# Attention and feed-forward in one kernel: batch 0 split into two pieces of its queries, with h of the first under the scores of the second

## The chip, the cores and the metric

The kernel runs on one core of a Trainium2 chip. The metric is the device time of one execution in microseconds. Before the change the median was 387.45 us over three runs (387.23 to 388.66). A program of one core has no second die to compare with; all runs that are compared here were in the fast state, that is, within 1.5% of the fastest run of their kernel. Some of them had a slightly lower mean granted TensorE clock than others (0.99 against 1.00), which is said where it matters.

Names in the profile: PE is TensorE, PEld its weight loads, DVE VectorE, ACT ScalarE, POOL GpSimd, SP SyncE.

## The reference

```python
def reference(q, k, v, w_in, w_out):            # q, k, v: 8 x 12 x 448 x 64
    scores = q @ k.transpose(0, 1, 3, 2) / 8
    attn = np.maximum(scores, 0.0) ** 2 / 448
    x = (attn @ v).transpose(0, 2, 1, 3).reshape(3584, 768)
    h = x @ w_in                                # 768 x 2048
    g = np.maximum(h, 0.0) ** 2
    return g @ w_out                            # 2048 x 768
```

There are eight batches of 448 rows. A batch is three units of four heads; a unit's keys come in J = 7 tiles of 64, so a batch has 21 score tiles. h of a batch can't start before its last unit's values are summed, since h sums over all heads.

## The kernel before

Each score tile is four 64x64 matmuls that run at the same time in the four quarters of the PE array. ACT takes relu out of PSUM, DVE squares, and a "value round" of four 64x64 matmuls adds the tile to the unit's output. `visit` is the unit of interleaving: scores of two tiles, then the value rounds of tiles seen two visits earlier. An f tile is 128 of the 2048 columns of h. In the lines of the profile, slot is a PSUM slot, at a score tile after its relu, avt the sum of the value rounds in PSUM, xt the transposed x, hps an accumulator of h, and g the squared relu of h.

```python
def slot(dtype):                       # a PSUM slot of two banks
    slot_no[0] += 1
    third = "mm" not in big and slot_no[0] % 3 == 2 and slot_no[0] < 29
    return (third_p if third else s_p).tile([P, 2, 2048 // size(dtype)], ...)

def score(t, times=1):
    ps = slot(FP32)
    for hh in list(range(2)) * times:  # times is 2 before h exists: the same product twice
        for hp in range(2):
            nc.tensor.matmul(ps[c, hh, 0:S], lhsT=kT[r, j, c], rhs=qT[r, :, c], ...)
    at = at_p.tile([P, 2, S], FP16, ...)
    nc.scalar.activation(out=at, in_=ps[:, :, 0:S], func=AF.Relu, scale=SK)

def visit(tiles, turn=None, lag=2, most=3):
    ...                                # prefetch of later units
    for t in tiles:
        score(t, 1 if "mm" in big else 2)
    later = pe_transpose(turn) if turn is not None else None
    flush()                            # squares on DVE
    av_some(lag, most)                 # value rounds
    ...
```

While batch 0's scores are made there are three slots. Then the third one's two banks become the two accumulators of h, and scores and transpositions share two slots. `pe_transpose` turns q and k of a unit on PE into one slot; copies to SBUF (qT, kT) follow, on DVE for units 0 to 2 and on ACT for units 3 to 5. Later units are transposed by DMA. The beginning is written out by hand, and h of batch 0 is then interleaved with the attention of batch 1:

```python
warm(10)
pe_transpose(0)
for i in range(11):
    visit([t for t in (2 * i, 2 * i + 1) if t < NB0], turn={1: 1, 4: 2, 10: 3}.get(i))
    ...                                # loads of later units and of the weights
f0 = h_group(0, 0)
for _, fn, _ in f0[0:4]:
    fn()
av_some(0, 9)
visit([NB0, NB0 + 1])
seq = [[2, 3], 4, [4, 5], [6, 7], [8, 9], 5, [10, 11], ...]   # visits and transpositions,
...                                    # one behind each of h's 16 groups of 6 matmuls
```

## Time and profile before

| stretch of the kernel before | from, us | to, us |
|---|---|---|
| batch 0's scores, until h goes on without a break | 8.2 | 29.66 |
| h of batch 0 under the attention of batch 1 | 29.66 | 61.38 |
| everything from h of batch 1 on | 61.38 | 385.6 |

The prediction below shows the lines behind the first two rows. The times of the second and third row are starts of h matmuls in the timeline of PE, the third of this one (start, us, then engine, line, operation, tiles, shapes and count):

```profile
61.38 0.93 PE L343 MATMUL hps<-xt,w 128*128 128x448 f16 x4
```

The last row is the same program in both kernels.

### The profile page before, as it was taken

To read this page: it belongs to the slowest core of one execution; us is meant where nothing else is said; L and a number is where in the kernel's file an instruction comes from. 1 tells how busy PE (TensorE), PEld (TensorE's weight loads), DVE (VectorE), ACT (ScalarE), POOL (GpSimd) and SP (SyncE) were. 2 spreads that over 40 slices of the span, in tenths; PEclk is the share of its full clock that TensorE was granted. 3 is DMA by queue.
4 is the path that set the end of the run, shared out by engine and by line. 5 is a ranking of instruction groups with operands and counts; after the bars stand their busy time and mean duration, and the time that the engine had idled before them with its cause. 6 is when DMAs were issued, how large, how long until landed. Compare 5 with 4: busy or idle time off the path is not lost.

```text
span 385.6 us, 7681 instructions
## 1 busy us (share of the span) xinstructions
PE 373.8 (97%) x3160; PEld 187.4 (49%) x3160; DVE 249.8 (65%) x401; ACT 235.9 (61%) x354; POOL 81.2 (21%) x96
## 2 busy tenths in 40 slices
PE   7889999999999999999999999999999999999994
PEld 3554434444554444445555544444555444556652
DVE  2885778999787676568587465566777563244441
ACT  3998874776555886676455578777464684442221
POOL 8544304653203222020113332030000000000001
PEclk9999999999999999999999999999999999999999
DMA  8999995998687994640989757344323300001333
GB/s 122 201 202 205 252 204 150 233 283 193 182 170 191 234 139 125 144 73 2 210 210 174 149 185 168 49 120 73 62 69 83 82 2 0 2 0 45 96 95 94
DMA packets 64482, 50.83 MB, mean 132 GB/s; under 512 B 35712, under 2 KB 60768, under 8 KB 64448
## 3 DMA queue, kind: packets, MB, share of 16 engines
q1 hardware_dynamic: 46672, 33.66, 36.0%
q0 software_dynamic: 17696, 16.58, 26.6%
q8 instruction: 25, 0.41, 0.4%
q10 hardware_dynamic: 80, 0.10, 0.1%
q14 instruction: 9, 0.07, 0.1%
HBM read 45.61 MB, written 11.01 MB: 147 GB/s over the span
## 4 chain that ended last, share of the span: by engine, by line
PE 86%; DVE 6%; ACT 3%; DMA 2%; issue 1%; POOL 1%; POOLq 0%; DVEq 0%; ACTq 0%
PE hps L343 38%; PE ops L497 27%; PE slot L248 9%; PE avt L266 7%; PE slot L497 4%; DVE at L312 2%; ACT at L252 2%; DMA k<-in_k_dram 2%; DVE xt L279 1%; DVE s L403 1%; PE slot L218 1%; ACT qT L210 0%; DVE g L364 0%; ACT kT L210 0%; POOL q L93 0%
## 5 line engine op out<-in xcount | busy, mean ns | idle before, releaser
L343 PE MATMUL hps<-xt,w 128*128 128x448 f16 x768 | 154.3, 353 | 0.3 <-ACT xt L276 0.3
L252 ACT ACTIVATE at<-slot 128x896 f16<-128x896 f32 x168 | 144.1, 920 | 16.0 <-PE slot L248 16.0
L312 DVE TENSOR_TENSOR at<-at 128x896 f16<-128x896 f16 x168 | 106.1, 653 | 33.0 <-ACT at L252 32.4
L343 PEld LDWEIGHTS <-w 128*128 128x128 f16 x768 | 71.2, 98 | 78.2 <-issue 16.9
L358 ACT ACTIVATE g<-hps 128x448 f16<-128x448 f32 x120 | 65.4, 546 | 56.1 <-PE hps L343 51.2
L364 DVE TENSOR_TENSOR g<-g 128x896 f16<-128x896 f16 x63 | 42.6, 677 | 43.8 <-ACT g L358 43.6
L497 PEld LDWEIGHTS <-s 128*128 128x128 f16 x448 | 42.6, 98 | 33.8 <-issue 4.1
L248 PE MATMUL slot<-qT,kT 64*64 64x448 f16 x756 | 53.8, 359 | 1.6 <-ACT kT L210 0.5
L123 POOL CAST qs<-qf 128x896 f16<-128x896 f32 x18 | 20.1, 1115 | 155.9 <-DMA qf<-in_q_dram 120.5
L266 PE MATMUL avt<-at,vt 64*64 64x448 f16 x672 | 47.8, 350 | 1.1 <-DVE xt L279 1.1
L497 PEld LDWEIGHTS <-g 128*128 128x128 f16 x336 | 31.3, 98 | 27.1 <-issue 7.7
L497 PE MATMUL ops<-b,s 128*128 128x384 f16 x192 | 35.2, 326 | 0.9 <-DVE s L403 0.9
L497 PE MATMUL ops<-t,s 128*128 128x384 f16 x192 | 34.6, 326 | 0.2
L279 DVE TENSOR_SCALAR xt<-avt 128x448 f16<-128x448 f32 x46 | 26.6, 618 | 12.6 <-PE avt L266 12.6
L497 PE MATMUL ops<-b,g 128*128 128x384 f16 x192 | 34.7, 326 | 0.0
L425 ACT ACTIVATE u<-ops 128x384 f32<-128x384 f32 x24 | 11.8, 492 | 34.9 <-PE ops L497 25.1
L248 PEld LDWEIGHTS <-kT 64*64 64x64 f16 x756 | 16.5, 105 | 31.8 <-issue 28.5
L266 PEld LDWEIGHTS <-vt 64*64 64x64 f16 x672 | 19.9, 107 | 14.9 <-issue 4.4
L374 POOL DMA_DIRECT2D out_dram<-osb x2 | 1.1, 568 | 121.2 <-ACT osb L460 121.2
L123 POOL CAST ks<-kf 128x896 f16<-128x896 f32 x18 | 23.0, 1277 | 4.9 <-DMA kf<-in_k_dram 4.1
L429 DVE SCALAR_TENSOR_TENSOR osb<-ops,u 128x384 f32<-128x384 f32 x24 | 13.3, 554 | 14.4 <-ACT u L425 10.0
L403 DVE TENSOR_TENSOR s<-g 128x1024 f16<-128x1024 f16 x26 | 19.1, 736 | 0.1
(50 smaller groups left out, 173.2 us busy)
## 6 DMA issues: line engine op xcount, KB each, us to landing
out_dram<-osb SPq DMA_DIRECT2D x52, 192.0 KB, 2.9
qf<-in_q_dram SPq DMA_DIRECT2D x16, 448.0 KB, 5.1
kf<-in_k_dram SPq DMA_DIRECT2D x16, 448.0 KB, 5.8
vt<-in_v_dram POOLq DMA_DIRECT2D x24, 224.0 KB, 4.6
w<-in_moe_w_in_dram POOLq DMA_DIRECT2D x8, 384.0 KB, 11.7
b<-in_moe_w_out_dram POOLq DMA_DIRECT2D x4, 768.0 KB, 17.4
q<-in_q_dram POOLq DMA_DIRECT2D x6, 224.0 KB, 7.8
k<-in_k_dram POOLq DMA_DIRECT2D x6, 224.0 KB, 8.1
```

Source lines behind the costliest of these rows:

```text
L123: ins = nc.gpsimd.tensor_copy(t.rearrange("p j h d -> p h j d"), src.rearrange("p h (j d) -> p h j d", d=D))
L248: nc.tensor.matmul(ps[c, hh, 0:S], lhsT=kT[r, j, c], rhs=qT[r, :, c], start=True, stop=True)
L252: nc.scalar.activation(out=at, in_=ps[:, :, 0:S], func=AF.Relu, scale=SK)
L266: nc.tensor.matmul(ap[hp][64 * hh:64 * hh + 64, 0:S], lhsT=vt[r, hh, j * D:(j + 1) * D], rhs=at[r, hh, :], start=(j == 0), stop=(j == J - 1))
L279: nc.vector.tensor_scalar(out=dst, in0=ap[hp][:, 0:S], scalar1=CX, scalar2=None, op0=ALU.mult)
L312: nc.vector.tensor_mul(at, at, at)
L343: held[:] = [nc.tensor.matmul(cell[0][:, 0:S], lhsT=w1[f // 4][:, m, (f % 4) * P:(f % 4 + 1) * P], rhs=xts[b][:, m, :], start=(m == 0), st ...
L358: nc.scalar.activation(out=g[:, f % 2], in_=cell[0][:, 0:S], func=AF.Relu)
L364: nc.vector.tensor_mul(g, g, g)
L403: op(to[i], x, y)
L429: nc.vector.scalar_tensor_tensor(out=osb[row][:, c], in0=Y[0][:, cc], scalar=CO, in1=keep[nm][:, cc], op0=ALU.mult, op1=ALU.add)
L497: nc.tensor.matmul(acc[0][:, 0:HALF], lhsT=left()[:, f], rhs=right[:, f], start=(fresh and f == 0), stop=(f == KH - 1), skip_group_check=n ...
```

## The change: its intent and the diff

In the kernel before, PE has little of use to do while ACT takes batch 0's relus. The change makes scores of the first 256 queries for all heads first (HEAD). h of these queries can then start, and the scores of the other 192 queries (TAIL) are made under it. Two tiles of a piece share a slot (2 x 256 or 2 x 192 columns in a bank). h is done in 16 blocks of two f tiles and one piece, 12 matmuls each. The order of all visits and h blocks up to h of batch 1 is fixed by hand. All relus of HEAD's h blocks are on ACT; of TAIL's, every second one is on DVE.

```diff
+    WHOLE, HEAD, TAIL = (0, J), (0, 4), (4, J)
+    av_order: deque = deque()
+    for piece in (HEAD, TAIL):
+        av_order.extend((t, piece) for t in range(NU * J))
+    av_order.extend((t, WHOLE) for t in range(NU * J, NUN * J))
...
+    def score(parts, times=1):
         ps = slot(FP32)
+        used = sum(width(piece) for _, piece in parts)
...
+                    nc.tensor.matmul(
+                        ps[c, hh, o:o + w], lhsT=kT[r, j, c],
+                        rhs=qT[r, piece[0]:piece[1], c], start=True, stop=True)
...
+        nc.scalar.activation(out=atv, in_=ps[:, :, 0:used], func=AF.Relu, scale=SK)
...
+    hd, tl = pairs(0, HEAD, range(20)), pairs(0, TAIL, range(4))
+    order0 = hd[:3] + tl[:1] + hd[3:7] + tl[1:] + hd[7:] + [[(20, HEAD), (4, TAIL)]]
+    for i, parts in enumerate(order0):
+        visit([parts], turn={2: 1, 7: 2}.get(i))
...                                   # loads: w1's first blocks now before q, k of unit 3
+    run(h0[0:4])
+    av_some(0, 9)
+    visit(next(tails))
+    run(h0[4:])
+    h_head(1)
+    visit(next(tails))
+    h_head(2)
+    pe_transpose(3)
+    visit(next(tails))
+    h_head(3)
+    visit(next(tails))
...
+    h_head(4)
+    visit(next(b1))
+    h_head(5)
+    visit(next(b1))
+    pe_transpose(4)
+    h_tail(0)
+    for i in range(1, 6):
+        visit(next(b1))
+        if i == 4:
+            pe_transpose(5)
+        h_tail(i)
...                                   # h_head(6), h_head(7), h_tail(6), h_tail(7), a visit before each
```

More of the change, by code (lines that the diff above doesn't have):

```diff
@@ L191, in slot @@
         slot_no[0] += 1
-        third = "mm" not in big and slot_no[0] % 3 == 2 and slot_no[0] < 29
+        third = "mm" not in big and slot_no[0] % 3 == 1
         return (third_p if third else s_p).tile(
@@ L224, in pe_transpose @@
         qkt[n] = ts
-        if n == 3:
-            return lambda: (copy(0, 0), copy(1, 0))
         if n > 0:
@@ L229, in pe_transpose @@
             copy(1, n < 3)
-        return None
     xts: dict = {}
@@ L236, with width, av_round @@
     now = [0]
-    av_order: deque = deque(range(NUN * J))
     avt = [None]
-    def score(t, times=1):
-        n, j = divmod(t, J)
-        qT, kT = qkt[n]
-        ps = slot(FP32)
-        for hh in list(range(2)) * times:
-            r = slice(64 * hh, 64 * hh + 64)
-            for hp in range(2):
-                c = slice(64 * hp, 64 * hp + 64)
-                nc.tensor.matmul(
-                    ps[c, hh, 0:S], lhsT=kT[r, j, c], rhs=qT[r, :, c],
-                    start=True, stop=True)
-        at = at_p.tile([P, 2, S], FP16, name="at", tag="at")
-        nc.scalar.activation(out=at, in_=ps[:, :, 0:S], func=AF.Relu, scale=SK)
-        ats[t] = at
-        seen[t] = now[0]
-    def av_round(t):
+    WHOLE, HEAD, TAIL = (0, J), (0, 4), (4, J)
[3 more added lines that the diff above has]
+    av_order.extend((t, WHOLE) for t in range(NU * J, NUN * J))
+    def width(piece):
+        return (piece[1] - piece[0]) * PW
+    def score(parts, times=1):
+        ps = slot(FP32)
+        used = sum(width(piece) for _, piece in parts)
+        at = at_p.tile([P, 1024], FP16, name="at", tag="at")
+        atv = at[:, 0:2 * used].rearrange("p (g w) -> p g w", w=used)
+        o = 0
+        for t, piece in parts:
+            n, j = divmod(t, J)
+            qT, kT = qkt[n]
+            w = width(piece)
+            for hh in list(range(2)) * times:
+                r = slice(64 * hh, 64 * hh + 64)
+                for hp in range(2):
+                    c = slice(64 * hp, 64 * hp + 64)
+                    nc.tensor.matmul(
+                        ps[c, hh, o:o + w], lhsT=kT[r, j, c],
+                        rhs=qT[r, piece[0]:piece[1], c], start=True, stop=True)
+            ats[t, piece] = atv[:, :, o:o + w]
+            seen[t, piece] = now[0]
+            o += w
+        nc.scalar.activation(out=atv, in_=ps[:, :, 0:used], func=AF.Relu, scale=SK)
+        return at[:, 0:2 * used], parts
+    def av_round(t, piece):
         n, j = divmod(t, J)
         b, u = divmod(n, NU)
-        vt, at = vts[n], ats.pop(t)
+        w = width(piece)
+        z = piece[0] * PW
+        assert all((t, piece) not in parts for _, parts in due)
+        vt, at = vts[n], ats.pop((t, piece))
         if j == 0:
@@ L266, in av_round @@
                 nc.tensor.matmul(
-                    ap[hp][64 * hh:64 * hh + 64, 0:S],
+                    ap[hp][64 * hh:64 * hh + 64, 0:w],
                     lhsT=vt[r, hh, j * D:(j + 1) * D], rhs=at[r, hh, :],
@@ L270, in av_round, with av_some @@
         if j == J - 1:
-            if u == 0:
+            if b not in xts:
                 xts[b] = x_p.tile([P, NM, S], FP16, name="xt", tag="xt")
             for hp in range(2):
-                dst = xts[b][:, 2 * u + hp, :]
+                dst = xts[b][:, 2 * u + hp, z:z + w]
                 if b < 2 and u == NU - 1 and hp == 0:
                     nc.scalar.activation(
-                        out=dst, in_=ap[hp][:, 0:S], func=AF.Copy, scale=CX)
+                        out=dst, in_=ap[hp][:, 0:w], func=AF.Copy, scale=CX)
                 else:
                     nc.vector.tensor_scalar(
-                        out=dst, in0=ap[hp][:, 0:S],
+                        out=dst, in0=ap[hp][:, 0:w],
                         scalar1=CX, scalar2=None, op0=ALU.mult)
-    def av_some(lag=2, most=3):
-        done = 0
-        while av_order and done < most:
-            t = av_order[0]
-            if t not in seen or seen[t] > now[0] - lag:
+    def av_some(lag=2, most=3.1):
+        done = 0.0
+        while av_order:
+            key = av_order[0]
+            done += width(key[1]) / S
+            if done > most or key not in seen or seen[key] > now[0] - lag:
                 break
             av_order.popleft()
-            av_round(t)
-            done += 1
-            if t % J == J - 1:
+            av_round(*key)
+            if key[0] % J == J - 1:
                 break
@@ L303, in prefetch, with visit, whole @@
         dma_transpose(m)
-    copies: deque = deque()
     due: list = []
     def flush():
-        for at in due:
+        for at, _ in due:
             nc.vector.tensor_mul(at, at, at)
         due.clear()
-    def visit(tiles, turn=None, lag=2, most=3):
+    def visit(slots, turn=None, lag=2, most=3.1):
         now[0] += 1
-        for t in tiles:
-            if t % J == 0 and t >= NPE * J:
-                prefetch(t // J + 2)
-        for t in tiles:
-            score(t, 1 if "mm" in big else 2)
-        later = pe_transpose(turn) if turn is not None else None
+        for parts in slots:
+            for t, _ in parts:
+                if t % J == 0 and t >= NPE * J:
+                    prefetch(t // J + 2)
+        new = [score(parts, 1 if "mm" in big else 2) for parts in slots]
+        if turn is not None:
+            pe_transpose(turn)
         flush()
         av_some(lag, most)
-        if later:
-            later()
-        due.extend(ats[t] for t in tiles)
+        due.extend(new)
         if "mm" not in big:
             flush()
+    def whole(ts):
+        return [[(t, WHOLE)] for t in ts]
     gts: dict = {}
@@ L352, in run @@
                 g = gts[pr][:, f0:f0 + 2, z:z + S]
-                if b == 0 and (f % 2 == 1 or f == 0) and f < 14:
-                    nc.vector.tensor_scalar(
-                        out=g[:, f % 2], in0=cell[0][:, 0:S],
-                        scalar1=0.0, scalar2=None, op0=ALU.max)
-                else:
-                    nc.scalar.activation(
-                        out=g[:, f % 2], in_=cell[0][:, 0:S], func=AF.Relu)
+                nc.scalar.activation(
+                    out=g[:, f % 2], in_=cell[0][:, 0:S], func=AF.Relu)
                 flush()
-                if b == 0 and f == NF - 1:
-                    due.append(g)
-                elif f % 2 == 1:
+                if f % 2 == 1:
                     nc.vector.tensor_mul(g, g, g)
@@ L367, in h_group, with h_piece, step, run @@
         return [(0.1892, step(m), m == 0) for m in range(NM)]
+    def h_piece(piece, i):
+        w = width(piece)
+        z = piece[0] * PW
+        cell = [None]
+        def step(e, m):
+            def run():
+                if e == 0 and m == 0:
+                    cell[0] = big["mm"].tile([P, 512], FP32, name="hps", tag="mm")
+                f = 2 * i + e
+                held[:] = [nc.tensor.matmul(
+                    cell[0][:, e * w:(e + 1) * w],
+                    lhsT=w1[f // 4][:, m, (f % 4) * P:(f % 4 + 1) * P],
+                    rhs=xts[0][:, m, z:z + w], start=(m == 0), stop=(m == NM - 1))]
+                if e == 0 or m < NM - 1:
+                    return
+                if 0 not in gts:
+                    gts[0] = g_p.tile([P, NF, 2 * S], FP16, name="g", tag="g")
+                g = gts[0][:, 2 * i:2 * i + 2, z:z + w]
+                src = cell[0][:, 0:2 * w].rearrange("p (e w) -> p e w", w=w)
+                if piece == TAIL and i % 2 == 0:
+                    nc.vector.tensor_scalar(
+                        out=g, in0=src, scalar1=0.0, scalar2=None, op0=ALU.max)
+                else:
+                    nc.scalar.activation(out=g, in_=src, func=AF.Relu)
+                flush()
+                if piece == TAIL and i == NF // 2 - 1:
+                    due.append((g, ()))
+                else:
+                    nc.vector.tensor_mul(g, g, g)
+            return run
+        return [step(e, m) for e in range(2) for m in range(NM)]
     def store(row, osb, c, eng, eng2=None):
@@ L529, with pairs, run, h_head @@
     NB0 = NU * J
+    def pairs(b, piece, ts):
+        parts = [(b * NB0 + t, piece) for t in ts]
+        return [parts[i:i + 2] for i in range(0, len(parts), 2)]
     warm(10)
     pe_transpose(0)
-    for i in range(11):
-        visit([t for t in (2 * i, 2 * i + 1) if t < NB0],
-              turn={1: 1, 4: 2, 10: 3}.get(i))
-        if i == 0:
-            load16(3)
+    hd, tl = pairs(0, HEAD, range(20)), pairs(0, TAIL, range(4))
+    order0 = hd[:3] + tl[:1] + hd[3:7] + tl[1:] + hd[7:] + [[(20, HEAD), (4, TAIL)]]
+    for i, parts in enumerate(order0):
+        visit([parts], turn={2: 1, 7: 2}.get(i))
+        if i == 2:
             load_w1(0)
             load_w1(1)
+            load16(3)
+            load_w1(2)
+        if i == 4:
+            load16(4)
             load_v(3)
-        if i == 2:
-            load16(4)
-            load_w1(2)
+            load_w1(3)
             load_v(4)
-        if i == 5:
+        if i == 8:
             load16(5)
-            load_w1(3)
             load_v(5)
             load_qk(6, nc.gpsimd)
+    first.close()
+    big["mm"] = ctx.enter_context(tc.tile_pool(name="mmps", bufs=2, space=PSUM))
+    def run(steps):
+        for fn in steps:
+            fn()
+    def h_head(*ii):
+        for i in ii:
+            run(h_piece(HEAD, i))
+    def h_tail(*ii):
+        for i in ii:
+            run(h_piece(TAIL, i))
+    tl = pairs(0, TAIL, range(5, 21))
+    tails = iter([tl[i:i + 2] for i in range(0, 8, 2)])
+    b1 = iter([whole([NB0 + t for t in ts]) for ts in
+               [(2 * i, 2 * i + 1) for i in range(10)] + [(20,)]])
+    h0 = h_piece(HEAD, 0)
+    run(h0[0:4])
[9 more added lines that the diff above has]
+    visit(next(tails))
     load_v(6)
@@ L554 @@
     load_qk(7, nc.gpsimd)
-    first.close()
-    big["mm"] = ctx.enter_context(tc.tile_pool(name="mmps", bufs=2, space=PSUM))
-    f0 = h_group(0, 0)
-    for _, fn, _ in f0[0:4]:
-        fn()
+    h_head(4)
[6 more added lines that the diff above has]
+        visit(next(b1))
+        if i == 4:
+            pe_transpose(5)
+        h_tail(i)
+    visit(next(b1))
+    h_head(6)
+    visit(next(b1))
+    h_head(7)
+    visit(next(b1))
+    h_tail(6)
+    visit(next(b1))
+    h_tail(7)
+    visit([])
     av_some(0, 9)
-    visit([NB0, NB0 + 1])
     T_G = NM * 0.1892
@@ L570 @@
     events = []
-    seq = [[2, 3], 4, [4, 5], [6, 7], [8, 9], 5, [10, 11], [12, 13], [14, 15],
-           [16, 17], [18, 19], [20], []]
-    for i, ts in enumerate(seq):
-        at = (2.5 + i) * T_G
-        if isinstance(ts, int):
-            events.append((at, lambda n=ts: pe_transpose(n)))
-        else:
-            events.append((at, lambda ts=ts: visit([NB0 + t for t in ts])))
-    events.append((T_H, lambda: av_some(0, 9)))
     def ready():
@@ L597 @@
             ts = [t0 + 2 * i, t0 + 2 * i + 1]
-            events.append((at0 + i * gap, lambda ts=ts: visit(ts)))
+            events.append((at0 + i * gap, lambda ts=ts: visit(whole(ts))))
         at0 = end
@@ L601 @@
         events.append((at0 + 0.3 + i, lambda: visit([])))
-    steps = [(0.1892, None, False)] * 4 + f0[4:]
-    for f in range(1, NF):
-        steps += h_group(0, f)
+    steps = []
     for f in range(NF):
@@ L613 @@
         steps += o_steps(pr)
-    clock = 0.0
+    clock = T_H
     ev = deque(sorted(events, key=lambda e: e[0]))
```

## The prediction

> **What bounds the kernel now.** I began with the summary of engines and then cut the span into stretches, because the change touches only the beginning: everything from h of batch 1 on stands in the same order in both kernels. The columns are the stretch, its length, then busy time and instruction count of PE, PEld, DVE, ACT and POOL, the granted clock, the share of the DMA engines and GB/s.
>
> ```profile
> PE 373.8 (97%) x3160; PEld 187.4 (49%) x3160; DVE 249.8 (65%) x401; ACT 235.9 (61%) x354; POOL 81.2 (21%) x96
> ...
> 8.00:26.00 18.00, 15.30 (x285) 8.73 (x278) 15.02 (x28) 16.67 (x21) 9.28 (x14) 1.00 1.24 200
> 27.40:61.40 34.00, 32.85 (x337) 14.46 (x334) 22.82 (x42) 26.57 (x36) 8.96 (x12) 1.00 1.24 229
> 61.40:92.00 30.60, 29.77 (x228) 14.09 (x224) 30.32 (x37) 21.48 (x34) 17.97 (x16) 1.00 0.98 214
> ```
>
> Over the whole span PE is the bound. But from 8 to 26 us, where batch 0's scores are made, ACT is busy 16.67 of 18 us: each score is issued twice there, so half of PE's score time does nothing. From 27.4 to 61.4 (h of batch 0 with attention of batch 1) PE leads, and ACT has 7.4 us in hand. From 61.4 to 92 DVE is full.
>
> The chain that ended last (start, us, what) shows the handover:
>
> ```profile
> 4.77 6.12 DMA k<-in_k_dram
> ...
> 24.98 0.97 ACT at L252
> 26.00 0.97 PE slot L218 x28
> 26.97 0.50 PE avt L266 x8
> 27.47 0.86 PE hps L343 x4
> 28.33 0.75 PE avt L266 x12
> 29.08 0.53 ACT xt L276
> 29.66 2.81 PE hps L343 x14
> ...
> 35.15 0.92 ACT qT L210
> 36.07 0.82 ACT kT L210
> ```
>
> h proper starts only at 29.66 us. That is the time which the change attacks. The last two lines are a warning: after a transposition of q and k, ACT needs 1.74 us to copy both out, and scores wait for the PSUM slot.
>
> The timeline of the same stage gives pitches (start, us, engine, line, operation, count):
>
> ```profile
> 12.06 4.96 ACT L252 ACTIVATE at<-slot 128x896 f16<-128x896 f32 x6 [0.48 <-PE slot L248]
> ...
> 37.62 1.31 PE L343 MATMUL hps<-xt,w 128*128 128x448 f16 x6
> 38.86 0.57 PE L248 MATMUL slot<-qT,kT 64*64 64x448 f16 x8
> 39.26 0.55 PE L266 MATMUL avt<-at,vt 64*64 64x448 f16 x8
> 39.74 1.31 PE L343 MATMUL hps<-xt,w 128*128 128x448 f16 x6
> ```
>
> Six relus take 4.96 us; with one at 0.92, the pitch is (4.96-0.92)/5 = 0.81 us. A round of h, scores and values takes 39.74-37.62 = 2.12 us.
>
> **What the Trainium skill says.** "TensorE: Matmul & The Clock Gate", section Back-to-back issue gap, gives N/2.4+2.5 ns per warm matmul: 189 ns for 448 columns. The chain has 48 h matmuls in 9.24 us, 192 ns, so it agrees. Estimates from the formula: 109 ns for 256 columns, 82.5 for 192. No row of this trace has a full 128x128 matmul so narrow; weight loads are hidden at 448. "ScalarE: Activation LUTs", section What ACT_TABLE_LOAD costs, gives 186 ns + 0.833 ns per element with some 93 ns overlapping: 932 ns for 896, measured 920. "TensorEngine Tiling (Array Packing)", section Key Properties, says that changing the tiling mode drains TensorE. The round above agrees: its work is 6 x 0.189 + 4 x 0.19 = 1.89 us, so some 0.23 us of 2.12 is changing over. The same page, section PSUM Bottleneck, warns that PSUM evacuation may become the bottleneck: exactly the 8 to 26 us stretch.
>
> **The change part by part: until h starts.** Before, ACT has 21 relus at 0.81 = 17.0 us ahead of h. After, it has ten of 1024 elements, two of 768 and one of 896. Adding or taking 128 elements at 0.833 ns moves the pitch by 0.107, to 0.92 and 0.70: 9.2+1.4+0.8 = 11.4 us. So 5.6 us of ACT work leaves this stretch. ACT starts at 8.23 as before. But the new order puts little work between a transposition and its first use. After three relus (to about 11.1) PE stands in the transposition that waits for k of unit 1, landing at 10.93 (first line of the chain), so the filling tail slot reaches ACT only near 12.4: 1.2 us idle. DVE then copies qT and kT, until 12.7, and unit 1's scores follow (0.3 idle). Unit 2 does the same at about 17 to 19 (two gaps of some 0.65). My hand schedule ends ACT's last relu near 8.2+11.4+2.9 = 22.5 to 22.9. The square on DVE (0.6), the last value rounds (0.3), the two evictions (0.4) and the first tail values come before h can go on: 24.4 against 29.66 before, 5.3 us earlier. The new order of loads puts w1's first two blocks ahead of q and k of unit 3; with loads at about 0.2 MB per us I find each landing before its use, so DMA changes nothing.
>
> **After h starts.** What was not done before h must be done now. PE work before, from 29.66: 92 h matmuls 17.4, 19 scores 3.6, 21 value rounds 4.0, two transposed units at 0.93, 1.9: 26.9 us, which took 31.7 (h of batch 1 starts at 61.38), so 4.8 of change-overs and waits. After, from 24.4: h in 92 x 0.109 + 96 x 0.0825 = 18.0; 12 tail scores at 0.0825 = 1.0 and 17 tail value rounds 1.4; 21 scores 4.0 and 21 value rounds 4.0; three transposed units 2.8: 31.2 us. There are 15 visits and three transpositions, 18 x 0.23 = 4.1 us. Waits, by following the two PSUM slots: the scores directly behind the transposition of unit 3 need the slot which ACT empties 1.74 us later, about 1.5; units 4 and 5 lose 0.5 to 1 each, since ACT is now short. Together about 3. Sum: 24.4+31.2+4.1+3.0 = 62.7, which is 1.3 us later than 61.38.
>
> ACT checks this. From 24.4 it has eight tail relus (5.6), 21 relus (17.0), three pairs of copies (5.2), eight head relus of g, all its own, at 0.49 (3.9), four of tail (1.5) and an eviction: 33.6 of 38.3 us, where before it was 26.57 of 34. Moving ACT's work later also moved it onto PE's busy stretch. PE's useful work is the same in all; what can be won is only its idle time and the duplicated scores, and much of the 5.3 us was already being used for transposing unit 3, for value rounds and for scores of batch 1.
>
> **After h of batch 0.** Nothing is added or removed there: the stretch up to 92 is DVE's in both. The difference at the start of h of batch 1 should carry to the end.
>
> **Rivals.** First: the waits in the interleaved stage are hidden, since the order was evidently set with care, and the first stretch runs with ACT full. Then 3 us of waits shrink to 1 and h starts at 23.5: 59.8, a gain of 1.6, 385.9. For it: before, ACT lost little at the same transpositions in the first stretch. Against: there, several relus stood between. Second: the narrow matmuls are paced by weight loads (98 ns in the trace) rather than by columns. Then tail h costs 96 x 0.0155 = 1.5 more: 390. Against: at 128 columns the transposes, with 64-wide weights, already run 14 in about 0.4 us. Third: a late load. DMA share is 1.24 until 60 us, and the bytes are the same, so backlog ends at 62 to 64 either way; if unit 6's transposition through DMA then runs late, 1 to 2 us are lost, up to 391.
>
> **Range and chances.** My schedule says +1.3 on 387.45. I shade to +0.8, because hand schedules overcount waits and because the order looks tuned: 388.2. Each of start of h, waits and pacing may be off by about 1.5 us; together 2 to 2.5: 385.8 to 390.8. Two per cent is 7.7 us, more than the whole earlier start of h, and a loss of 7.7 would need several rivals at once. Faster 0.01, same 0.97, slower 0.02.
>
> **What would show it.** Right: full h blocks from 24 to 25 us; h of batch 1 starting 61 to 64; ACT over 85% busy in between; a PE wait of over 1 us behind unit 3's copies; unchanged duration from there on. Wrong: h matmuls of 192 columns over 90 ns apart, w1 or k as releaser of PE, DVE busier than ACT in the interleaved stage, or a late stage of another length.

## The result, and the profile after

The changed kernel is right and took 390.09 us in the median of four runs (388.66 to 390.53), beside 387.34 us of the kernel before (four runs now). The ratio is 1.0061 with a 95% interval from 1.0034 to 1.0088. Ratios are the mean time of one kernel's fast runs over that of the other's of the same rounds, so they are not quite the ratio of the medians. The change makes the kernel some 0.6% slower.

First the stretches, cut at the points where h goes on and where h of batch 1 starts (columns as in the prediction). The kernel after:

```profile
8.00:24.90 16.90, 13.37 (x385) 10.09 (x384) 12.12 (x22) 13.10 (x16) 8.65 (x14) 1.00 1.23 196
24.90:64.20 39.30, 35.70 (x559) 25.36 (x558) 27.19 (x58) 34.22 (x48) 10.50 (x14) 1.00 1.17 214
64.20:94.80 30.60, 29.67 (x227) 14.08 (x224) 29.95 (x36) 21.37 (x33) 17.43 (x16) 1.00 1.02 212
```

The kernel before, cut in the same way:

```profile
8.00:29.70 21.70, 18.75 (x345) 10.59 (x338) 16.84 (x30) 19.79 (x25) 11.69 (x18) 1.00 1.24 200
29.70:61.40 31.70, 30.80 (x309) 13.55 (x309) 22.21 (x41) 24.60 (x33) 7.42 (x10) 1.00 1.24 230
```

The first stretch is 4.8 us shorter, as the change means it to be. The second is 7.6 us longer, and ACT is busy 34.22 of its 39.3 us where it was busy 24.60 of 31.7. In the third, cut to the length that it has before, DVE is as full as it was. h of batch 1 now starts here:

```profile
64.16 1.12 PE L361 MATMUL hps<-xt,w 128*128 128x448 f16 x5
```

The whole rest takes the same time in the two profiled runs: 388.3 - 64.16 = 324.1 us after, 385.6 - 61.38 = 324.2 before. The loss is made before 64.2 us.

That the rest is so equal is in part chance. In both runs PE waits 0.94 us for a sum that DVE makes. In the chain of the kernel after:

```profile
93.42 1.35 DVE s L449
94.81 1.47 PE ops L543 x8
```

PE's wait at this place is between nothing and 1.46 us in the fourteen traces of this study (none in the control below, 1.46 in e1_space3), and the rest is 322.9 to 324.6 us long, mostly in step with it. The sum that PE waited for took 1.41 us in the kernel after and 0.69 in the control; the traces do not show why. So traces are compared by the start of h of batch 1, and not by their ends.

In the chain that ended last of the kernel after (start, us, what), the handover and two of three transpositions:

```profile
21.96 0.93 ACT at L268
22.91 0.64 DVE at L328
...
24.96 2.29 PE hps L391 x20
...
30.96 0.92 ACT kT L211
32.45 1.42 PE hps L391 x12
...
51.75 0.92 ACT kT L211
...
64.23 9.19 PE hps L361 x48
```

Copies of kT were on the chain before too (the prediction's lines show one at 36.07 us), in the middle of a stage that should belong to PE. The list of who waited for whom, for PE alone and in the second stretch, says how much they cost. Columns: who, for whom, us in total, times, longest. Before:

```profile
PE slot L248 <- ACT kT L210: 0.5, 2, 0.3
PE avt L266 <- DVE xt L279: 0.4, 2, 0.2
PE hps L343 <- ACT xt L276: 0.3, 1, 0.3
```

After:

```profile
PE slot L262 <- ACT kT L211: 2.3, 3, 1.5
PE slot L219 <- ACT at L268: 1.0, 2, 0.7
PE avt L284 <- DVE at L328: 0.2, 1, 0.2
```

PE waits 3.5 us instead of 1.2; and the last wait of the list before ended at 29.66 us, where the stretch begins, so that 0.9 of the 1.2 us lie inside it. The three waits of 2.3 us in all are for kT to leave its slot, the two of 1.0 us are transpositions that need a slot which ACT has not emptied yet. The longest one and the pace of narrow h matmuls stand in the timeline of PE (start, us, then as before; what ended an idle time stands in brackets):

```profile
30.04 0.36 PE L262 MATMUL slot<-qT,kT 64*64 64x192 f16 x8
31.93 0.36 PE L262 MATMUL slot<-qT,kT 64*64 64x192 f16 x8 [1.53 <-ACT kT L211]
...
43.32 1.17 PE L391 MATMUL hps<-xt,w 128*128 128x192 f16 x12
44.41 0.57 PE L262 MATMUL slot<-qT,kT 64*64 64x448 f16 x8
```

The second score slot of a visit starts 1.89 us after the first, since the transposition stands right ahead of it. A block of twelve 192-column matmuls takes 44.41 - 43.32 = 1.09 us. Their starts lie 82 or 83 ns apart in the trace (109 at 256 columns), which makes 0.99, and 0.1 is left for the ends of the block, where the tiling mode changes. Weight loads of 98 ns do not pace it.

So the sum of the second stretch is, before, 26.9 us of work + 0.9 of waits + 3.9 of the rest, which I take for change-overs; after, 31.2 + 3.5 + 4.6. (The work is the prediction's count, the waits are the lists' inside the stretch, the rest is what is left of 31.72 and 39.26 us.) The differences, 4.3 + 2.6 + 0.7, less the 4.76 us by which h goes on earlier, make the 2.8 us.

### The profile page after: what moved, and what is told of

Same layout as the page of the kernel before. It is cut to its first block, busy times and chain, and to the rows that moved or that the text cites. A ratio compares the mean times of both kernels' runs of the same rounds, so it can differ in the third digit from the quotient of the medians.

```text
span 388.3 us, 8278 instructions
## 1 busy us (share of the span) xinstructions
PE 373.4 (96%) x3444; PEld 198.8 (51%) x3444; DVE 250.4 (65%) x410; ACT 238.6 (61%) x359; POOL 78.2 (20%) x96
## 4 chain that ended last, share of the span: by engine, by line
PE 84%; DVE 7%; ACT 4%; DMA 2%; issue 2%; POOLq 0%; POOL 0%; ACTq 0%
PE hps L361 33%; PE ops L543 25%; PE slot L262 9%; PE avt L284 7%; PE slot L543 4%; PE hps L391 4%; DVE at L328 3%; ACT at L268 3%; DVE s L449 2%; PE slot L219 1%; DMA q<-in_q_dram 1%; ACT kT L211 1%; DMA out_dram<-osb 1%; DVE xt L297 1%; DVE kT L213 0%
## 5 line engine op out<-in xcount | busy, mean ns | idle before, releaser
L268 ACT ACTIVATE at<-slot 128x896 f16<-128x896 f32 (+2 forms) x168 | 144.9, 920 | 15.7 <-PE slot L262 15.6
L361 PE MATMUL hps<-xt,w 128*128 128x448 f16 x672 | 133.5, 353 | 0.0
L328 DVE TENSOR_TENSOR at<-at 128x896 f16<-128x896 f16 (+2 forms) x168 | 108.4, 663 | 37.2 <-ACT at L268 36.5
L361 PEld LDWEIGHTS <-w 128*128 128x128 f16 x672 | 63.0, 98 | 67.0 <-issue 12.0
L371 ACT ACTIVATE g<-hps 128x448 f16<-128x448 f32 x112 | 60.9, 545 | 52.5 <-PE hps L361 47.6
L375 DVE TENSOR_TENSOR g<-g 128x896 f16<-128x896 f16 x56 | 36.2, 647 | 43.4 <-ACT g L371 43.3
L262 PE MATMUL slot<-qT,kT 64*64 64x448 f16 (+2 forms) x860 | 52.6, 330 | 3.7 <-ACT kT L211 2.3
L284 PE MATMUL avt<-at,vt 64*64 64x448 f16 (+2 forms) x756 | 48.2, 330 | 2.5 <-DVE at L328 2.1
L297 DVE TENSOR_SCALAR xt<-avt 128x448 f16<-128x448 f32 (+2 forms) x51 | 27.2, 571 | 11.9 <-PE avt L284 11.8
L391 PE MATMUL hps<-xt,w 128*128 128x256 f16 (+1 forms) x192 | 21.2, 260 | 0.0
```

The lines of the kernel that those rows point to most:

```text
L262: nc.tensor.matmul(ps[c, hh, o:o + w], lhsT=kT[r, j, c], rhs=qT[r, piece[0]:piece[1], c], start=True, stop=True)
L268: nc.scalar.activation(out=atv, in_=ps[:, :, 0:used], func=AF.Relu, scale=SK)
L284: nc.tensor.matmul(ap[hp][64 * hh:64 * hh + 64, 0:w], lhsT=vt[r, hh, j * D:(j + 1) * D], rhs=at[r, hh, :], start=(j == 0), stop=(j == J - 1))
L297: nc.vector.tensor_scalar(out=dst, in0=ap[hp][:, 0:w], scalar1=CX, scalar2=None, op0=ALU.mult)
L328: nc.vector.tensor_mul(at, at, at)
L361: held[:] = [nc.tensor.matmul(cell[0][:, 0:S], lhsT=w1[f // 4][:, m, (f % 4) * P:(f % 4 + 1) * P], rhs=xts[b][:, m, :], start=(m == 0), st ...
```

## The experiments

Each kernel ran in five rounds beside the kernel before. "h of batch 1" is the start of its first matmul in the trace. All gave right results.

| run | median, us | before in the same call | ratio, 95% interval | h of batch 1, us |
|---|---|---|---|---|
| c0_control (the change) | 389.69 | 386.65 | 1.0086 (1.0061 to 1.0110) | 63.85 |
| e1_space3 | 388.77 | 386.65 | 1.0047 (1.0030 to 1.0065) | 62.65 |
| e2_dve_relu | 390.32 | 386.65 | 1.0094 (1.0081 to 1.0107) | 64.70 |
| e3_tails_first | 392.80 | 386.65 | 1.0155 (1.0137 to 1.0174) | 67.75 |
| e5_192_256 | 391.09 | 387.27 | 1.0091 (1.0059 to 1.0123) | 67.95 |
| e6_split_copies | 389.24 | 387.27 | 1.0046 (1.0027 to 1.0066) | 63.50 |
| e7_tails_first_twice | 392.36 | 387.27 | 1.0136 (1.0099 to 1.0174) | 69.22 |
| e4_old_loads | 390.12 | 387.27 | 1.0064 (1.0042 to 1.0086) | 63.90 |
| e8_dve_copies | 388.09 | 386.88 | 1.0037 (1.0023 to 1.0051) | 61.87 |
| b1_all | 387.44 | 386.88 | 1.0010 (0.9999 to 1.0022) | 61.83 |
| b2_before_dve | 388.97 | 386.88 | 1.0070 (1.0046 to 1.0093) | 62.46 |
| b3_space3_dve | 387.47 | 387.28 | 1.0006 (0.9992 to 1.0020) | 61.52 |

Single runs scatter: the control's six go from 388.64 to 391.69, and its two slowest have a mean granted clock of 0.994 and 0.996. In the first call the kernel before scatters less (386.29 to 387.54 in eleven runs), in the second as much (386.32 to 390.30 in 35). The trace shows only one run of each, for the control its fastest. So a trace's difference and a ratio's need not agree to better than about 1 us. Nor do ratios of different calls, which ran on different chips: the changed kernel itself had 1.0061 when it was first measured and 1.0086 as the control. Runs with the same time before (386.65, 387.27, 386.88, 387.28) are of one call, and the control is of the first.

### c0_control: the changed kernel again

> The changed kernel again, on the same chip as the three beside it. Expected: 2 to 3 us over the kernel before (ratio 1.005 to 1.008); h blocks without a break from about 24.9 us; h of batch 1 from about 64.2 us.

The ratio 1.0086 lies a little above the expected 1.005 to 1.008, and h of batch 1 starts at 63.85 us, 0.35 earlier than expected. h goes on at 24.58 us instead of 24.9.

### e1_space3: unit 3's transposition between two h blocks

```diff
     run(h0[4:])
+    visit(next(tails))
     h_head(1)
     visit(next(tails))
     h_head(2)
     pe_transpose(3)
-    visit(next(tails))
     h_head(3)
     visit(next(tails))
```

> Unit 3's transposition now has an h block on both sides, so that ACT can copy qT and kT out while PE works; nothing else is added or taken away. My theory (PE waits for the PSUM slots that ACT empties): the wait of 1.53 us behind kT goes, h of batch 1 starts at 62.5 to 63.0 and the kernel is 1.2 to 1.7 us faster than the control, so 1 to 1.6 us over the kernel before. Rival (ACT's total work is the bound of the stage, the place of its waits does not matter): under 0.5 us faster than the control, the wait turning up elsewhere.

The timeline of PE in this run, at the place of the 1.53 us wait:

```profile
30.07 0.56 PE L219 MATMUL slot<-ident,k 128*64 128x128 f16 x14
30.56 1.48 PE L391 MATMUL hps<-xt,w 128*128 128x256 f16 x12
31.98 0.83 PE L262 MATMUL slot<-qT,kT 64*64 64x192 f16 x16
```

There is an h block where the wait was, and no bracket behind the scores. h of batch 1 starts 63.85 - 62.65 = 1.20 us earlier, and by the ratios the run is 0.0039 x 386.65 = 1.5 us faster than the control (0.6 us if the control's two slowest runs are left out). The theory holds for the start of h of batch 1: the place of the transposition mattered, with the work of every engine unchanged. The gain is not safe until the end: in this profiled run PE's wait for DVE at 93.7 us, 1.46 us, took it back, and the span is 387.2 us beside the control's 386.9.

### e2_dve_relu: less work for ACT, the order unchanged

```diff
-                if piece == TAIL and i % 2 == 0:
+                if i % 2 == 0:
                     nc.vector.tensor_scalar(...)
```

> Every second relu of the first piece's h goes from ACT to DVE: four of 0.49 us pitch (2.0 us) less on ACT, four of about 0.68 us more on DVE. If ACT's total is the bound of the interleaved stage: 1 to 2 us faster than the control. If only the ordering behind the transpositions costs: within 0.4 us of the control, since three of the four relus do not stand before a transposition.

It is not faster than the control (1.0094 and 1.0086, and h of batch 1 0.85 us later in the trace). PE still waits 1.53 us for kT behind unit 3, though ACT is busy 32.16 us between the two starts of h, where it is 34.23 in the control. Of the 0.85 us, 0.33 come from h going on later (24.91 us; PE had waited longer for k of unit 1). The rest is lost near 60 us, where value rounds stand behind evictions that DVE, with the added relu, makes later. So less work for ACT did not pay here, but the run does not part that from what it cost on DVE. Together with e1_space3, where no engine's work changed and 1.20 us were won, the rival falls.

### e3_tails_first: no overlap of tail scores and h

```diff
-    run(h0[0:4])
     av_some(0, 9)
-    visit(next(tails))
-    run(h0[4:])
-    h_head(1)
-    visit(next(tails))
-    h_head(2)
-    pe_transpose(3)
-    visit(next(tails))
-    h_head(3)
-    visit(next(tails))
+    for t_ in range(4):
+        visit(next(tails))
+    run(h0)
+    h_head(1)
+    h_head(2)
+    pe_transpose(3)
+    h_head(3)
```

> All scores of the second piece are made before any h; h is still in pieces. This undoes the overlap that the change is for. (Unit 3's transposition has h blocks on both sides, as in the run that spaces it, so it is to be read against that one.) If the overlap is worth what it seems (eight tail relus of 0.70 us, six of them uncovered, 4.2 us): 4 us slower than the spaced run. My theory, that the stage after it then has less to do (12 scores, 17 value rounds, three visits with their changes of tiling mode: about 1.0 + 0.8 + 0.7 us): 1 to 2 us slower than the spaced run, so about level with the control.

My expectation was wrong, and the other one was right: the run is (1.0155 - 1.0047) x 386.65 = 4.2 us slower than the spaced run. The stretches show a part of it that I had not thought of:

```profile
24.00:27.00 3.00, 2.04 (x56) 1.30 (x56) 1.63 (x5) 2.53 (x5) 1.70 (x3) 0.98 1.25 207
27.00:30.00 3.00, 2.64 (x56) 2.01 (x59) 2.51 (x6) 3.00 (x5) 0.70 (x1) 0.50 1.25 204
30.00:33.00 3.00, 3.00 (x31) 2.05 (x21) 1.14 (x3) 0.55 (x1) 2.04 (x3) 0.50 1.25 206
```

While PE waited for ACT between short groups of matmuls, the granted clock (third column from the end) fell to half, and stayed so after h had begun. That the waits were the cause is not shown. The first 36 h matmuls took 5.55 us, where 36 x 109 ns are 3.9. h started at 30.58, 6.0 us after the spaced run's 24.59, where I had reckoned with some 4.2. The work saved afterwards was as I had reckoned: 67.75 - 30.58 = 37.2 us, less the 1.6 lost to the clock, is 35.5, against 38.1 in the spaced run, so 2.5 less. 6.0 - 2.5 + 1.6 gives the 5.1 us between the two traces.

### e7_tails_first_twice: the same with doubled scores

```diff
-    def visit(slots, turn=None, lag=2, most=3.1):
+    def visit(slots, turn=None, lag=2, most=3.1, twice=False):
...
-        new = [score(parts, 1 if "mm" in big else 2) for parts in slots]
+        new = [score(parts, 1 if "mm" in big and not twice else 2) for parts in slots]
...
-        visit(next(tails))
+        visit(next(tails), twice=True)
```

> As the run with all second-piece scores before h, but these scores are issued twice, as those of the first stretch are, so that PE is kept busy while ACT works. In the run without this the granted clock from 20 to 64 us was 0.92. If that slow clock was a part of its loss: clock back at 1.00 and the time about 1.5 to 2.5 us below that run, so 2 to 3 us over the spaced run (ratio to the kernel before about 1.010 to 1.012). If the loss was all ACT's uncovered work: level with it (1.0155).

This is inconclusive on the clock. In the profiled run k of unit 1 landed late (PE's transposition of it started at 11.91 us, in the control at 10.58), and the granted clock was 0.50 between 30 and 33 us all the same. Three of the six runs had a mean clock of 0.999 or 1.000 and took 391.60, 391.99 and 392.73 us. The ratio's interval, 1.0099 to 1.0174, covers both expectations. What the two runs together do show: without the overlap the kernel is 3.4 us (1.0136) to 4.2 us (1.0155) slower than the spaced run. The overlap, the idea of the change, is worth that much within the split form, with what the slower clock cost in those runs (1.6 us in e3_tails_first's trace) counted in.

### e5_192_256: the smaller piece first

```diff
-    WHOLE, HEAD, TAIL = (0, J), (0, 4), (4, J)
+    WHOLE, HEAD, TAIL = (0, J), (0, 3), (3, J)
...
     h_head(5)
-    visit(next(b1))
+    visit(next(b1), most=4.1)
     pe_transpose(4)
```

Without the second edit the check found that h of the second piece read an output not yet written; it was mended before it ran.

> The pieces the other way round: 192 queries first, 256 second (and the value rounds of one visit allowed up to 4.1 tiles, so that the second piece's last are done before its h). ACT's relus ahead of h fall from about 11.4 to 9.7 us, so h should go on 1.5 to 1.9 us earlier, near 23. Theory (what leaves the first stretch comes back in the interleaved one: eight tail relus of 0.92 instead of 0.70 us, wider tail scores and value rounds): h of batch 1 starts within 0.8 us of the control's 63.9, the time within 0.2% of it. Rival (the start of h sets the time): 1.5 us or more faster than the control, ratio to the kernel before under 1.005.

The profile fell on a disturbed run. In its timeline of PE:

```profile
12.42 0.96 PE L219 MATMUL slot<-ident,k 128*64 128x128 f16 x14 [2.88 <-DMA k<-in_k_dram]
```

PE stood still for 2.88 us for unit 1's k, the clock was 0.57 from 12 to 16 us, and h went on only at 27.83. So its stages say nothing about the split. Of the times, 1.0091 with an interval from 1.0059 is not under 1.005, and its fastest run took 389.76 us, the control's 388.64: the split did not gain the 1.5 us that the rival expects. But the rival, that an earlier start of h is all that counts, is not tested by that, since no trace shows h starting earlier. Whether a clean run would start h at 23 us stays open.

### e6_split_copies: one copy on each engine

```diff
         if n > 0:
-            copy(0, n < 3)
+            copy(0, 1)
             copy(1, n < 3)
```

> Only the engine of one copy is changed: for units 3, 4 and 5 qT is copied out of PSUM by DVE and kT by ACT, at the same time, where ACT did both one after the other (1.74 us). Theory (PE waits for PSUM slots behind these copies): of the waits behind kT in the control (1.53, 0.40, 0.41 us) the first falls to about 0.7 and the others go, h of batch 1 starts near 62.3, and the kernel is 1.3 to 1.9 us faster than the control. Rival (the waits are only shown there, ACT or DVE are behind anyway): under 0.5 us.

The experiment did not do what it was made for. In the timeline of ACT:

```profile
30.59 0.92 ACT L211 ACTIVATE kT<-slot 128x896 f16<-128x896 f16 x1 [1.03 <-DVE qT L213]
```

ACT's copy of kT was made to wait for DVE's copy of qT from the same PSUM tile, so the pair was still done one after the other and the slot came free only 0.09 us sooner (PE waited 1.44 instead of 1.53). h of batch 1 moved by 0.35 us. That agrees with the theory, but does not test it. The ratio, 1.0046, looks like the gain that was expected, 1.5 us on the control; with next to nothing changed in the trace, it rather shows what ratios of two calls are worth.

### e4_old_loads: the old order of the loads

```diff
-            load_w1(0)
-            load_w1(1)
             load16(3)
-            load_w1(2)
+            load_w1(0)
+            load_w1(1)
+            load_v(3)
...
-            load_v(3)
-            load_w1(3)
+            load_w1(2)
             load_v(4)
...
             load16(5)
+            load_w1(3)
             load_v(5)
```

> The changed kernel with the old order of the loads (q, k of unit 3 and v of unit 3 before w1's first blocks). By the theory loads are never waited for in either order: within 0.3 us of the control. Rival (the new order of loads earns or costs something): more than 0.7 us away from it, with w as releaser of PE near 22 us.

h of batch 1 starts at 63.90 us, 0.05 from the control's, and no load of weights is a releaser of PE. The ratios (1.0064 and 1.0086, in different calls) overlap in their intervals. The order of loads neither earns nor costs anything that these runs can show.

### e8_dve_copies: both copies on DVE

```diff
         if n > 0:
-            copy(0, n < 3)
-            copy(1, n < 3)
+            copy(0, 1)
+            copy(1, 1)
```

> What the run with split copies was meant to do and did not (there the ACT copy was made to wait for the DVE copy of the same PSUM tile, so the slot came free no sooner): both copies of units 3, 4 and 5 go to DVE, which takes about 0.62 + 0.54 us for the pair instead of 1.74 and is nearly free behind a transposition. Theory (PE waits for the slot): the wait behind unit 3's copies falls from 1.53 to about 1.0 us, the two of 0.40 go, those of 0.34 and 0.69 ahead of the transpositions fall or stay; h of batch 1 near 62.4, 1.2 to 1.8 us faster than the control. Rival (DVE pays with its squares and the waits move there): under 0.6 us faster.

In the timeline of DVE, the copies of unit 3:

```profile
29.67 0.62 DVE L213 COPY qT<-slot 128x896 f16<-128x896 f16 x1
30.20 0.61 DVE L213 COPY kT<-slot 128x896 f16<-128x896 f16 x1
```

The pair takes 1.14 us instead of 1.72. PE's wait behind unit 3 fell to 0.91 us (ended now by a relu's slot on ACT), both waits of 0.40 went, and those ahead of units 4 and 5 stayed at 0.34 and 0.69. h of batch 1 starts at 61.87, 1.98 earlier than the control's, of which 0.23 is an earlier start of h (24.35). The ratio is 0.0049 lower, 1.9 us, but in another call. By the trace the theory holds again.

### b1_all: everything found so far

```diff
-        visit([parts], turn={2: 1, 7: 2}.get(i))
+        visit([parts], turn={2: 1, 6: 2}.get(i), lag=3 if i == 11 else 2)
...                                   # with the edits of e1_space3 and of e8_dve_copies
```

> Everything found so far in one: unit 3 between two h blocks, the copies of units 3 to 5 on DVE, unit 2 transposed one visit earlier, and the value rounds of one visit in the first stretch put off by a visit, so that they do not stand before scores that ACT waits for. Theory: h goes on at about 23.8 instead of 24.6; of the waits only some 1.2 us are left; h of batch 1 near 60.5 to 61.0 and the time 0.3 to 1.0 us below the kernel before (ratio 0.997 to 1.000). Rival (the split costs more in narrow pieces and changes of mode than it can win): ratio 1.001 or more.

Level with the kernel before (interval 0.9999 to 1.0022) and not better. The ratio, 1.0010, lies where the rival's range began, and h of batch 1 at 61.83 us is later than the 60.5 to 61.0 of the theory. The two edits of the first stretch failed in the profiled run: h went on at 25.21 us, later than in the control. k of unit 1 landed 0.5 us later there, which explains a part; and the transposition, put earlier, stood ahead of value rounds that then waited 1.24 us for evictions behind its copies on DVE. How the 0.6 us divide was not tested.

### b2_before_dve: the copies of the kernel before on DVE

The diff is that of e8_dve_copies, in the kernel before; there it changes units 4 and 5 only.

> The kernel before with one edit: the copies of units 4 and 5 go from ACT to DVE. Theory (the waits for the slot, 0.26 us twice, are in that kernel too, but an h block already hides most of the copying): 0.3 to 0.7 us faster, ratio 0.998 to 0.999. Rival: DVE's queue takes it back, ratio 1.000.

It is slower: 1.0070, and h of batch 1 starts 1.08 us later (in the trace of its fastest run; the ratio stands for 2.7 us). The timeline of DVE says why:

```profile
35.73 0.62 DVE L364 TENSOR_TENSOR g<-g 128x896 f16<-128x896 f16 x1
36.26 0.62 DVE L212 COPY qT<-slot 128x896 f16<-128x896 f16 x1
36.80 0.61 DVE L212 COPY kT<-slot 128x896 f16<-128x896 f16 x1
```

The transposition ended at about 34.98 us (34.42 + 0.56), but the copies stand in DVE's queue behind squares of scores and of g, and PE's wait for kT grew from 0.26 to 0.93 us. The rival was right, and by more than I had allowed. The same edit helps one order of instructions and hurts the other: what counts is which engine's queue is empty when the transposition ends.

### b3_space3_dve: the two edits that took waits away

This is e1_space3 and e8_dve_copies together.

> The two edits that each removed a wait, alone together: unit 3 between two h blocks and the copies of units 3 to 5 on DVE; the two edits of the first stretch are left out, since they did not make h go on earlier. By adding: h of batch 1 at 61.87 less the 0.91 us wait that is left behind unit 3, so about 61.0 us, 0.4 before the kernel before's 61.38: ratio 0.998 to 1.000. If the waits only move on: 61.8 and ratio 1.001 to 1.003.

All waits behind kT are gone. Of the timeline's waits of PE after h has started, these two are left, and one of 0.23 us at the end:

```profile
38.32 0.58 PE L219 MATMUL slot<-ident,q 128*64 128x128 f16 x14 [0.34 <-ACT at L268]
47.84 0.58 PE L219 MATMUL slot<-ident,q 128*64 128x128 f16 x14 [0.70 <-ACT at L268]
```

h of batch 1 starts at 61.52 us, between the two expectations, with h going on at 24.90 as in the changed kernel's first profile. The waits fell from 3.5 to 1.27 us, 64.16 - 61.52 = 2.6 us were won back, and the kernel is level with the one before (0.9992 to 1.0020). No kernel of this study is shown to be faster than the kernel before.

## Why the prediction was right or wrong

**The whole.** The time, 390.09, lies in the range (385.8 to 390.8) near its upper end, and the class, within 2%, was right. The middle, 388.2, was 1.9 us low. The unshaded sum, +1.3 us, had the right direction; the measured one is +2.7 (medians).

**What bounds the kernel.** Right. The stretch until h is shorter with less ACT work ahead of it, and from h of batch 1 on nothing was edited. The prediction had DVE's stretch in it, but not that PE's wait for DVE at its end differs from run to run (0 to 1.46 us), so that in a single run a difference at h of batch 1 carries to the end only to within a good microsecond.

**Until h starts.** Predicted 24.4 us, measured 24.90. There are gaps in ACT where I expected them, but their sizes were wrong: the trace of ACT has idle times of 0.26, 0.32, 0.49, 0.66 and 0.44 us between its relus, 2.2 in all where I had 2.8. The largest, 1.2 us behind k of unit 1, is the 0.26: k kept PE waiting for 0.15 us only. On the other hand ACT began at 8.58 and not at 8.23 us. Its last relu ended at 22.88 us, inside my 22.5 to 22.9, in part by luck, and h went on 2.0 us after it, where I had 1.5 to 1.9.

**After h starts.** Predicted 31.2 + 4.1 + 3.0; the waits measured 3.5, and with the same count of work, 31.2, 4.6 are left for change-overs. The mechanism is right, and each size but the counted work was a little low: h's start by 0.5, change-overs by 0.5, waits by 0.5. Of the single waits, unit 3's was predicted at 1.5 and measured at 1.53; units 4 and 5 cost 0.74 and 1.10 us where I had said 0.5 to 1 each.

**The shading.** Wrong. I took 0.5 us off, because hand schedules overcount waits and the order looked tuned. This one undercounted them. e1_space3 and e8_dve_copies show that the order was not tuned at these places.

**"ACT checks this."** The prediction put ACT at 33.6 us of work in the stage, and the trace has 34.22 busy. But the conclusion that could be drawn from it, that ACT's fullness is the cause, is refuted by e1_space3 and e2_dve_relu together. The waits come from when ACT empties certain slots. The prediction had both readings, and only the order of slots is borne out.

**The rivals.** The first (waits hidden, ACT full in the first stretch, 385.9) did not happen; b3_space3_dve, where most waits are hidden, reaches only the kernel before. The second (weight loads pace narrow matmuls) is refuted by starts 82 or 83 ns apart, 1.09 us per block of twelve. The third (a late load in the later stage) did not occur in the profiled run: the wait at 94.81 us is for DVE, and it was there before; nor did the order of the loads matter in e4_old_loads. A late k of unit 1, in the first stretch, does occur in single runs (12.42 us in e5_192_256's profile), which the prediction did not have.

**Where the gain went.** In the first stretch PE is idle for 21.70 - 18.75 = 2.95 us before and for 16.90 - 13.37 = 3.53 after. Duplicated scores are, by the prediction's rates, 21 x 0.19 = 4.0 us before and 21 x 0.109 + 5 x 0.0825 = 2.7 after. That is 6.95 us without use before and 6.2 after: an estimate, but it says why an earlier h brings so little. The stretch became shorter by 4.8 us mostly because useful work left it, 4.1 us by this count, and that work came back in the next stretch. What was truly saved, about 0.7 us, is less than what the new waits (2.6) and the further change-overs (0.7) cost. The loss of the waits is shown by experiment; that of the change-overs is only counted.

**Open.** What makes single runs of one kernel differ by 3 to 4 us was not settled: traces show one run each. PE's wait for DVE near 94 us, 0 to 1.46 us, is one source, in both kernels; whether late loads, with a clock that falls behind them, are another was not tested.

## What to carry to other kernels

When a change lets a stage start earlier, ask first how much unused time of the limiting engine it removes; work that only moves to a later, fuller stage has to be done there. Where two PSUM slots serve both transpositions and scores, put a block of other matmuls on both sides of a transposition, and choose the copying engine by whose queue is empty at that moment, not by whose total is smaller.

## What the Trainium skill lacked or had wrong

- "TensorE: Matmul & The Clock Gate", section Back-to-back issue gap, adds to its formula that a real kernel's sustained spacing at 512 columns is about 131 ns, so that the formula over-counts there. Here 48 matmuls of 448 columns took 9.24 us, 192 ns each, which is the formula's 189 ns and not less. The formula holds at 192 columns too, with a new 128x128 weight for each matmul: the starts lie 82 or 83 ns apart, and twelve take 1.09 us, change-over included.
- No page says that a copy out of PSUM can be made to wait for another engine's copy from another bank of the same tile (qT and kT each fill part of one bank of the slot); in e6_split_copies it was, for 1.03 us. The traces do not show whether the chip needs this or only the program's own tracking of tiles put it there.
